# The second FFN's weight conversions in two parts, one more of them in the first group, and the last four turns in two pairs

## The chip, the cores and the metric

The program runs on one core of a Trainium2 chip. The core has a matrix engine (PE, with its weight loads shown as PEld), a vector engine (DVE), a scalar engine (ACT), a third elementwise engine that also issues gathers (POOL), and a queue engine that issues transfers (SP). The metric is the device time of one execution in microseconds (us), the median of several.

## What is computed

Three stages follow one another. The input of the third stage is x, 4608 tokens of 512 numbers, and its weights are an FFN of 2048 hidden numbers.

```
attn:  kv = k^T v per head; out = q kv; out / rms(out) * g_norm      (8 x 8 heads, 576 tokens, 64)
moe:   tokens with x @ w_skip > 0 go to one of 8 experts e:
       y = gate * (max(x @ w1[e], 0) @ w2[e]);  x = x + y             (512 -> 1024 -> 512)
moe2:  h = x @ w_in;  g = h * sigmoid(h);  out = g @ w_out            (512 -> 2048 -> 512)
```

## The kernel before, in words

Every float32 matrix product is made of three products of reduced-precision parts: high by high, high by low, low by high. So each weight and each activation is first split into two parts. The order of all work is written out by hand: each engine takes its instructions in the order in which the code issues them, and waits at the head of its queue.

The change lies in one loop, `for n in range(len(steps) + LAG)` (line 1554 on). Steps 0 to 63 are the eight experts `u` = 0 to 7 with eight weight chunks `f` = 0 to 7 each. Steps 64 to 111 are three groups of 512 tokens in the second FFN, with sixteen chunks each. A step does, in this order:

- in the experts, at `f` = 5, 6, 6, 7 one **turn** each (`turn`, line 1207): PE transposes a quarter of the next expert's rows into a PSUM tile `pt`, ACT copies the high part (L1215), DVE subtracts for the low part (L1216). There are two `pt` tiles, so the transposes of the third turn wait for the L1216 of the first. In the last expert all four turns stand at `f` = 7;
- `first` (line 1290): PE's first product of the step into `ph` (L1303), from which ACT and DVE make the two parts of the hidden tile `h` (L1309 and L1310 for an expert, L1315 to L1317 for a group);
- `split_on` (line 213): the end of the conversions that have begun, see below;
- `second` (line 1346) of the step before: PE's second product into `acc` (L1355). It needs `h` of the step before. After an expert's last chunk, DVE adds `acc` to the rows `xe` (L1365), and POOL stores them and gathers the rows of the expert after the next (L967);
- the step's preparation of later weights (`split`, line 182). An expert's chunk is one ACT copy (L187) and one DVE subtraction (L188). Half a chunk of the second FFN comes as 64-bit numbers and is **converted**: L197 on ACT and five DVE operations, L198, L200, L202, L206 and L210; later `split_on` issues an ACT copy L221, two POOL operations L222 and L223, and then a DVE addition L218.

Which half is converted at which expert step is said by the table `at_step`; the halves that remain are converted by `split_slowly(LAST_OPS)`, which advances the generator `split` by so many yields in a step of the groups. Loads of the weights run three ahead in three `stg` buffers, in the order of the conversions. Temporary tiles of a conversion (`x1`, `x2`, `x3`) are of the pool `xp` with six buffers.

Of the kernel before, what the change touches and what calls it, by code (L numbers as in the profile page):

```python
# [24 lines left out]
def tile_kernel(ctx, tc, q, qr, k, kr, v, vr, g_norm, w_skip, w_gate, we, wf, out):  # L25
    nc = tc.nc
    B, _, H, _, D = k.shape
    NT, DM = out.shape
    S = NT // B
    E, KE = we.shape[:2]  # L30
# [12 lines left out]
    KD = DM // P  # L43
# [9 lines left out]
    NW = 16  # L53
    NWE = 5
# [39 lines left out]
    NE = E * KE  # L94
# [81 lines left out]
    def part(task):  # L176
        c, half = task
        w = chunk_tile(c)
        return w if half is None else w[:, :, half * DM:(half + 1) * DM]

    def split(task):


        t = staged.pop(task)
        w = part(task)
        if task[1] is None:
            nc.scalar.activation(w[:, 0, :], t.bitcast(F32), AF.Copy)  # L187
            nc.vector.tensor_tensor(w[:, 1, :], t.bitcast(F32), w[:, 0, :].bitcast(F32), ALU.subtract)  # L188
            yield
            return  # L190
        tv = t.rearrange("p (n o) -> p n o", o=2)
        hi, lo = tv[:, :, 1], tv[:, :, 0]
        vec = nc.vector
        x1 = xp.tile([P, DM], F32, tag="x", name="x1")
        x3 = xp.tile([P, DM], F32, tag="x", name="x3")
        x2 = xp.tile([P, DM], F32, tag="x", name="x2")
        nc.scalar.activation(x3, lo.bitcast(U32), AF.Copy, scale=2.0 ** -52)  # L197
        vec.tensor_scalar(x2.bitcast(I32), hi, 0x7FFFFFFF, None, ALU.bitwise_and)  # L198
        yield
        vec.scalar_tensor_tensor(x1, x2, SMALLEST, hi.bitcast(F32), ALU.is_ge, ALU.mult)  # L200
        yield
        vec.tensor_scalar(  # L202
            x2.bitcast(I32), x1.bitcast(I32), 3, 0x3FFFFFFF, ALU.logical_shift_left, ALU.bitwise_and
        )
        yield
        vec.scalar_tensor_tensor(  # L206
            x1.bitcast(I32), x1.bitcast(I32), -0x40000000, x2.bitcast(I32), ALU.bitwise_and, ALU.bitwise_or
        )
        yield
        vec.tensor_scalar(x2.bitcast(I32), x1.bitcast(I32), -0x800000, None, ALU.bitwise_and)  # L210
        begun.append((w, x1, x2, x3))
        yield
# [12 lines left out]

    NCW = 2 * (NW - NWE)
    at_step = {}
    for n in range(NE - NWA):  # L230
        at_step.setdefault(n + 1, []).append((n + NWA, None))
    for i in range(NCW):
        n = (i // 3) * KE + 2 + 2 * (i % 3) if i < NCW - 1 else NE - KE - 1
        at_step.setdefault(n, []).append((NE + i // 2, i % 2))

    LAST_OPS = 4
    order = [(c, None) for c in range(NWA)] + [x for n in sorted(at_step) for x in at_step[n]]
    order += [(NE + i // 2, i % 2) for i in range(NCW, 2 * KF)]
    nload = [0]
    nsplit = [0]  # L240

    def load_ahead():
        while nload[0] < min(nsplit[0] + 3, len(order)):
            load_task(order[nload[0]])
            nload[0] += 1

    def split_next(n):
        for _ in range(n):
            for _ in split(order[nsplit[0]]):
                pass  # L250
            nsplit[0] += 1
            load_ahead()

# [22 lines left out]
    with ExitStack() as actx:  # L276
# [583 lines left out]
        for nb in range(3, B):  # L860
            o = {3: 2, 4: 1}.get(nb, 0)
            for i, parts in enumerate(((0, 1), (2, 3), (4,), (5,))):
                b, u = (nb - 1, o + i) if o + i < 4 + (nb - 1) % 2 else (nb, 0)
# [110 lines left out]
    for u, (kind, i) in enumerate(units):  # L974
        n = CAPS[i] if kind == "e" else GN
# [46 lines left out]
    with ExitStack() as vctx:  # L1022
        oc = vctx.enter_context(tc.tile_pool(name="oc", bufs=1))
        ps_v = vctx.enter_context(tc.tile_pool(name="ps_v", bufs=1, space=PSUM))
        with tc.For_i(0, count, 1) as _:
            vec = nc.vector
            _, _, over = reach(oc)
# [10 lines left out]
            at = oc.tile([P, NTILE, E], F32, name="at")  # L1038
# [162 lines left out]
    def turn_tile(u, kk, s, pt):  # L1201
        m = tokens_of[u][s]
        c0 = kk * (XQ if u < E else P)
        nc.tensor.transpose(pt[:, s * P:s * P + m], rows_of[u][s][0:m, c0:c0 + P], ident[0:m, 0:m])  # L1204

    def turn(u, kk, pt=None):
        if pt is None:
            pt = ps_t.tile([P, GN], F32, tag="t", name="pt")
            for s in range(len(tokens_of[u])):
                turn_tile(u, kk, s, pt)  # L1210
        if kk % 2 == 0:
            two_x[0] = xtp.tile([P, 2, 2, GN], F32R, tag="xT", name="xT")
        x = two_x[0][:, :, kk % 2]
        n = sum(tokens_of[u])
        nc.scalar.activation(x[:, 0, 0:n], pt[:, 0:n], AF.Copy)  # L1215
        nc.vector.tensor_tensor(x[:, 1, 0:n], pt[:, 0:n], x[:, 0, 0:n].bitcast(F32), ALU.subtract)  # L1216
        xT_of[u, kk] = x
# [77 lines left out]
    def first(u, f, c):  # L1295
        kind, _ = units[u]
        n = sum(tokens_of[u])
        w = chunks[c]
        ph = ps_h.tile([P, GN], F32, tag="h", name="ph")
        for kk in range(KD):  # L1300
            x = xT_of[u, kk]
            for a, (wi, xi) in enumerate(((0, 0), (0, 1), (1, 0))):
                nc.tensor.matmul(  # L1303
                    ph[:, 0:n], w[:, wi, kk * P:(kk + 1) * P], x[:, xi, 0:n],
                    start=(kk == 0 and a == 0), stop=(kk == KD - 1 and a == 2),
                )
        h = hp_.tile([P, 2, GN], F32R, tag="h", name="h")
        if kind == "e":
            nc.scalar.activation(h[:, 0, 0:n], ph[:, 0:n], AF.Relu)  # L1309
            nc.vector.scalar_tensor_tensor(  # L1310
                h[:, 1, 0:n], ph[:, 0:n], 0.0, h[:, 0, 0:n].bitcast(F32), ALU.max, ALU.subtract
            )
        else:
            sg = sgp.tile([P, GN], F32, tag="sg", name="sg")
            nc.scalar.activation(sg, ph, AF.Silu)  # L1315
            nc.scalar.activation(h[:, 0, :], sg, AF.Copy)  # L1316
            nc.vector.tensor_tensor(h[:, 1, :], sg, h[:, 0, :].bitcast(F32), ALU.subtract)  # L1317
        return h
# [243 lines left out]
    for n in range(len(steps) + LAG):  # L1562
        now = steps[n] if n < len(steps) else None
        if now is not None:
            u, f, c = now
            kind, i = units[u]
            nxt = u + 1
            if u < E:
                at = (5, 6, 6, 7) if u != E - 1 else (7, 7, 7, 7)
                for kk in range(KD):  # L1570
                    if at[kk] == f:
                        turn(nxt, kk)
            hs[n] = first(u, f, c)
        else:
            sup = super_group(0)
            for _ in range(2):
                next(sup)
        split_on()
        if n >= LAG:
            u2, f2, c2 = steps[n - LAG]  # L1580
            second(u2, f2, c2, hs.pop(n - LAG))
            last = f2 == nf[units[u2][0]] - 1
            if last and u2 + 2 <= E:
                fetch(u2 + 2)
            if u2 == E + NPL - 1 and f2 >= KF - NWE:
                load_entry(f2 - (KF - NWE))
        split_next(len(at_step.get(n, [])))
        if n >= NE:
            split_slowly(LAST_OPS)
        if now is not None and E <= u < E + NPL - 1:  # L1590
            if f < 2 * GT:
                fetch_blocks(nxt, f)
            if f >= KF - GT - 1 and f < KF - 1:
                turn_blocks(nxt, f - (KF - GT - 1))
        if now is not None and u == E + 1:
            keep_part(c, 0)
            keep_part(c, 1)
        if n >= NE + KF and (n - NE - KF) % 3 == 0 and (n - NE - KF) // 3 < KJ:
            sums_now.append(sums_of((n - NE - KF) // 3))
        for _ in range(2):  # L1600
            step_on(sums_now)
        if now is not None and u == E + NPL - 1:
            if f in (9, 10, 11, 12):
                pace(rooms[0][0])
            for v in (E + NPL, E + NPL + 1):
                if f < 4:
                    fetch_blocks(v, f)
                elif f in (9, 10, 11, 12):
                    fetch_blocks(v, f - 5)
            if f in (8, 10, 12, 14):  # L1610
                rooms.append([xp.tile([P, DM], F32, tag="x", name="room") for _ in range(4)])
                parts.append(operand_parts(E + NPL, f // 2 - 4, rooms[-1]))
            for _ in range(2):
                step_on(parts)
            assert f < KF - 1 or not parts
        if now is not None and nxt == E and f == at[0] - 1:
            sort_rows(nxt)
        if n == 0:
            row_of_place()
        elif n % 2 == 0 and n // 2 <= NP:  # L1620
            permute(n // 2 - 1)
        if n == 31:
            prepare_blocks()
        if n == 32:
            order_blocks()
        if n == 24:
            nc.sync.dma_start(inew, perm.rearrange("(p t) c -> p t c", p=P))
# [61 lines left out]
```

## Time and profile before

| what | value |
|---|---|
| median of 3 runs | 1195.29 us (1193.83 to 1196.43) |
| profiled execution | 1185.35 us, span 1183.3 us, mean granted PE clock 0.978 |
| PE busy | 1131.6 us (96%) |
| DVE, ACT, POOL busy | 595.2 us (50%), 484.0 us (41%), 368.8 us (31%) |
| experts (steps 0 to 63) | 141 to 406 us of the span |
| first group (steps 64 to 79) | about 406 to 491 us of the span |

The span is from the first instruction to the last. PE is the engine with hardly any idle time; what counts is therefore where PE waits and for whom. The other engines are idle for half the time on the average, but they work in bursts, and what they finish late can hold PE. Granted clock 1.00 is 2.4 GHz, 0.50 is 1.2 GHz.

### The profile page before, as it was taken

To read this page: it belongs to the slowest core of one execution; us is meant where nothing else is said; L and a number is where in the kernel's file an instruction comes from. 1 tells how busy PE (TensorE), PEld (TensorE's weight loads), DVE (VectorE), ACT (ScalarE), POOL (GpSimd) and SP (SyncE) were. 2 spreads that over 40 slices of the span, in tenths; PEclk is the share of its full clock that TensorE was granted. 3 is DMA by queue.
4 is the path that set the end of the run, shared out by engine and by line. 5 is a ranking of instruction groups with operands and counts; after the bars stand their busy time and mean duration, and the time that the engine had idled before them with its cause. 6 is when DMAs were issued, how large, how long until landed. Compare 5 with 4: busy or idle time off the path is not lost.

```text
span 1183.3 us, 16638 instructions
## 1 busy us (share of the span) xinstructions
PE 1131.6 (96%) x6259; PEld 939.5 (79%) x6259; DVE 595.2 (50%) x1105; ACT 484.0 (41%) x951; POOL 368.8 (31%) x369
## 2 busy tenths in 40 slices
PE   8895699999998999989999999999999999999998
PEld 7785698888886888868878788888888888888886
DVE  2467677788888577624535522355222453223222
ACT  3575354445444443422423444433244432344221
POOL 3679344535444186150063234120043200000000
PEclk9897799999999999999999999999999999999999
DMA  9867656666665433094641376432566322654202
GB/s 341 329 259 296 222 166 210 223 218 210 224 209 200 161 108 115 14 309 155 208 143 54 127 265 216 176 124 91 182 219 221 141 107 104 217 189 170 104 36 71
DMA packets 65265, 211.05 MB, mean 178 GB/s; under 512 B 9840, under 2 KB 24688, under 8 KB 53024
## 3 DMA queue, kind: packets, MB, share of 16 engines
q1 hardware_dynamic: 55760, 189.44, 45.8%
q0 software_dynamic: 8064, 20.48, 5.9%
q8 instruction: 50, 0.82, 0.3%
q10 hardware_dynamic: 1360, 0.05, 0.1%
q14 instruction: 31, 0.25, 0.1%
HBM read 162.67 MB, written 47.27 MB: 177 GB/s over the span
## 4 chain that ended last, share of the span: by engine, by line
PE 87%; DVE 5%; issue 3%; DMA 2%; ACT 2%; POOL 1%; SPq 0%; POOLq 0%; DVEq 0%; ACTq 0%
PE acc L1498 22%; PE acc L1355 19%; PE ph L1303 19%; PE pa L1451 11%; PE pc L1451 6%; PE pb L1451 3%; PE po L456 2%; PE kv L424 1%; PE pt L1204 1%; DVE w L188 1%; POOL x L223 1%; PE kv L426 1%; PE busy L1120 1%; PE G L445 0%; DMA xs<-rows 0%
## 5 line engine op out<-in xcount | busy, mean ns | idle before, releaser
L1355 PE MATMUL acc<-w,h 128*128 128x512 f32 x1128 | 282.4, 397 | 10.7 <-issue 5.5
L1303 PE MATMUL ph<-xT,w 128*128 128x512 f32 (+7 forms) x1344 | 265.8, 347 | 0.8 <-DVE w L188 0.4
L1498 PE MATMUL acc<-entry,h 128*128 128x512 f32 x1152 | 265.1, 392 | 0.0
L1498 PEld LDWEIGHTS acc<-entry,h 128*128 128x128 f32 x1152 | 216.3, 188 | 47.9
L1355 PEld LDWEIGHTS acc<-w,h 128*128 128x128 f32 x1128 | 203.4, 183 | 60.8 <-issue 7.5
L1303 PEld LDWEIGHTS ph<-xT,w 128*128 128x128 f32 x1344 | 225.3, 189 | 30.8 <-DVE w L188 0.7
L1001 POOL DMA_INDIRECT x<-xs,qidx x128 | 128.2, 1002 | 112.8 <-DVE room L1266 48.8
L1451 PE MATMUL pa<-b,entry 128*128 128x512 f32 x576 | 141.8, 393 | 0.0
L1479 DVE TENSOR_TENSOR h<-g,h 128x512 fp32r<-128x512 f32 x96 | 66.5, 693 | 147.8 <-ACT h L1478 145.4
L1451 PEld LDWEIGHTS pa<-b,entry 128*128 128x128 f32 x576 | 108.2, 188 | 24.8
L1478 ACT ACTIVATE h<-g 128x512 fp32r<-128x512 f32 x96 | 60.5, 630 | 146.6 <-PE acc L1498 141.5
L1317 DVE TENSOR_TENSOR h<-sg,h 128x512 fp32r<-128x512 f32 x48 | 34.8, 726 | 119.4 <-ACT h L1316 81.0
L188 DVE TENSOR_TENSOR w<-stg_None,w 128x1024 fp32r<-128x1024 f32 x64 | 80.3, 1256 | 17.3 <-ACT w L187 15.7
L1433 ACT ACTIVATE g<-g 128x512 f32<-128x512 f32 x72 | 45.4, 633 | 103.1 <-DVE g L1431 91.0
L1315 ACT ACTIVATE sg<-ph 128x512 f32<-128x512 f32 x48 | 28.7, 597 | 141.7 <-PE ph L1303 102.4
L222 POOL TENSOR_TENSOR x<-x,x 128x512 f32<-128x512 f32 x32 | 41.6, 1299 | 111.3 <-DVE x L210 106.1
L1451 PE MATMUL pc<-b,entry 128*128 128x512 f32 x288 | 74.3, 393 | 0.0
L1309 ACT ACTIVATE h<-ph 128x304 fp32r<-128x304 f32 (+6 forms) x64 | 28.0, 437 | 109.0 <-PE ph L1303 97.1
L187 ACT ACTIVATE w<-stg_None 128x1024 fp32r<-128x1024 f32 x64 | 67.1, 1049 | 9.8 <-DMA xs<-rows 9.8
L1451 PEld LDWEIGHTS pc<-b,entry 128*128 128x128 f32 x288 | 54.1, 188 | 12.4
L223 POOL TENSOR_TENSOR x<-x,w 128x512 f32<-128x512 f32 x32 | 62.9, 1966 | 0.6 <-ACT w L221 0.6
L1431 DVE TENSOR_TENSOR g<-pc,u 128x512 f32<-128x512 f32 x24 | 16.6, 692 | 73.0 <-PE pc L1451 73.0
(216 smaller groups left out, 1166.8 us busy)
## 6 DMA issues: line engine op xcount, KB each, us to landing
entry<-wa SPq DMA_DIRECT2D x42, 1024.0 KB
stg_None<-in_we_dram SPq DMA_DIRECT2D x64, 512.0 KB
entry<-wb SPq DMA_DIRECT2D x24, 1024.0 KB
stg<-in_wf_dram SPq DMA_DIRECT2D x32, 512.0 KB
xs<-rows SPq DMA_DIRECT2D x8, 1032.0 KB
wb<-w SPq DMA_DIRECT2D x16, 512.0 KB
wa<-parts SPq DMA_DIRECT2D x32, 256.0 KB
k<-in_k_dram SPq DMA_DIRECT2D x7, 1024.0 KB
```

The costliest lines, as they stand in the source:

```text
L187: nc.scalar.activation(w[:, 0, :], t.bitcast(F32), AF.Copy)
L188: nc.vector.tensor_tensor(w[:, 1, :], t.bitcast(F32), w[:, 0, :].bitcast(F32), ALU.subtract)
L222: nc.gpsimd.tensor_tensor(x3, x3, x2, ALU.mult)
L223: nc.gpsimd.tensor_tensor(x1, x1, w[:, 0, :].bitcast(F32), ALU.subtract)
L1001: nc.gpsimd.indirect_dma_start(out=rows_of[u][s][:, a * XQ:(a + 1) * XQ], out_offset=None, in_=xblocks, in_offset=bass.IndirectOffsetOnAxi ...
L1303: nc.tensor.matmul(ph[:, 0:n], w[:, wi, kk * P:(kk + 1) * P], x[:, xi, 0:n], start=(kk == 0 and a == 0), stop=(kk == KD - 1 and a == 2),)
L1355: nc.tensor.matmul(accs[u, s][0:m], h[:, hi, s * P:s * P + m], w[:, wi, DM:2 * DM], start=(f == 0 and a == 0), stop=(last and a == 2),)
L1433: nc.scalar.activation(g, acc, AF.Silu)
L1451: nc.tensor.matmul(p, w[:, wi, kk], x[:, xi, kk], start=(i in FIRST_IN_BANK and kk == 0 and a == 0), stop=(kk == 1 and a == 2), skip_group ...
L1478: nc.scalar.activation(h[:, 0], g, AF.Copy)
L1479: nc.vector.tensor_tensor(h[:, 1], g, h[:, 0].bitcast(F32), ALU.subtract)
L1498: nc.tensor.matmul(acc[ni, s], h[:, hi, s * P:(s + 1) * P], w[:, wi], start=(j == 0 and fi == 0 and a == 0), stop=(last and a == 2),)
```

## The change

Three things are changed. First, the table `at_step` holds 21 halves in place of 22, at `f` = 0, 2 and 4 of experts 0 to 6 (before: `f` = 2, 4, 6 and one more at step 55), and each is issued in two parts: ACT's L197 and DVE's L198, L200, L202 at its step, L206 and L210 at the next step (`split_at`). Second, eleven halves in place of ten are left for the first group, and `LAST_OPS` is 5 in place of 4, which is a whole conversion in each of the steps 64 to 74. Third, in the last expert two of the four turns go behind `first` of step 63.

```diff
-    NCW = 2 * (NW - NWE)
+    NCW = 2 * (NW - NWE) - 1
...
-        n = (i // 3) * KE + 2 + 2 * (i % 3) if i < NCW - 1 else NE - KE - 1
-        at_step.setdefault(n, []).append((NE + i // 2, i % 2))
-
-    LAST_OPS = 4
+        at_step.setdefault((i // 3) * KE + 2 * (i % 3), []).append((NE + i // 2, i % 2))
+
+    LAST_OPS = 5
...
+    parted = []
+
+    def split_at(n):
+
+        while parted:
+            for _ in parted.pop():
+                pass
+        for task in at_step.get(n, []):
+            g = split(order[nsplit[0]])
+            if task[1] is None:
+                for _ in g:
+                    pass
+            else:
+                for _ in range(3):
+                    next(g)
+                parted.append(g)
+            nsplit[0] += 1
+            load_ahead()
...
-                for kk in range(KD):
+                for kk in range(KD if u != E - 1 else KD // 2):
                     if at[kk] == f:
                         turn(nxt, kk)
             hs[n] = first(u, f, c)
+            if u == E - 1 and f == at[0]:
+                for kk in range(KD // 2, KD):
+                    turn(nxt, kk)
...
-        split_next(len(at_step.get(n, [])))
+        split_at(n)
```

DVE's queue in expert 6 before, from the chunk subtraction of step 48 on (`w50` is an expert's chunk, `stg73_0` half a chunk of the second FFN, `h` a step's hidden tile):

```order
L188 TENSOR_TENSOR w50_4215<-stg50_None_4127,w50_4215 128x1024
L1310 SCALAR_TENSOR_TENSOR h_4233<-ph_4220,h_4233 128x288
L188 TENSOR_TENSOR w51_4248<-stg51_None_4138,w51_4248 128x1024
L1310 SCALAR_TENSOR_TENSOR h_4266<-ph_4253,h_4266 128x288
L188 TENSOR_TENSOR w52_4278<-stg52_None_4177,w52_4278 128x1024
L198 TENSOR_SCALAR x2_4286<-stg73_0_4218 128x512
L200 SCALAR_TENSOR_TENSOR x1_4284<-x2_4286,stg73_0_4218 128x512
L202 TENSOR_SCALAR x2_4286<-x1_4284 128x512
```

The same place now (line numbers of the changed kernel; its L1328 is L1310 of before):

```order
L188 TENSOR_TENSOR w50_4215<-stg50_None_4095,w50_4215 128x1024
L198 TENSOR_SCALAR x2_4223<-stg73_0_4141 128x512
L200 SCALAR_TENSOR_TENSOR x1_4221<-x2_4223,stg73_0_4141 128x512
L202 TENSOR_SCALAR x2_4223<-x1_4221 128x512
L1328 SCALAR_TENSOR_TENSOR h_4243<-ph_4230,h_4243 128x288
L206 SCALAR_TENSOR_TENSOR x1_4221<-x1_4221,x2_4223 128x512
L210 TENSOR_SCALAR x2_4223<-x1_4221 128x512
L188 TENSOR_TENSOR w51_4260<-stg51_None_4178,w51_4260 128x1024
L1328 SCALAR_TENSOR_TENSOR h_4278<-ph_4265,h_4278 128x288
L188 TENSOR_TENSOR w52_4293<-stg52_None_4218,w52_4293 128x1024
```

The conversion has moved two steps up, and it stands on both sides of an `h`. Three of its operations now come right behind the additions to `xe`, which stand ahead of the first row.

DVE's queue at the start of the first group before, from `h` of step 65 to the conversion that begins at step 66:

```order
L1317 TENSOR_TENSOR h_4833<-sg_4834,h_4833 128x512
L210 TENSOR_SCALAR x2_4811<-x1_4809 128x512
L198 TENSOR_SCALAR x2_4862<-stg75_1_4669 128x512
L200 SCALAR_TENSOR_TENSOR x1_4860<-x2_4862,stg75_1_4669 128x512
L202 TENSOR_SCALAR x2_4862<-x1_4860 128x512
L1317 TENSOR_TENSOR h_4882<-sg_4883,h_4882 128x512
L218 TENSOR_TENSOR w75_4808<-x1_4809,x3_4810 128x512
L206 SCALAR_TENSOR_TENSOR x1_4860<-x1_4860,x2_4862 128x512
L210 TENSOR_SCALAR x2_4862<-x1_4860 128x512
```

The same place now (its L1335 is L1317 of before):

```order
L1335 TENSOR_TENSOR h_4818<-sg_4819,h_4818 128x512
L218 TENSOR_TENSOR w74_4373<-x1_4793,x3_4794 128x512
L198 TENSOR_SCALAR x2_4848<-stg75_0_4654 128x512
L200 SCALAR_TENSOR_TENSOR x1_4846<-x2_4848,stg75_0_4654 128x512
L202 TENSOR_SCALAR x2_4848<-x1_4846 128x512
L206 SCALAR_TENSOR_TENSOR x1_4846<-x1_4846,x2_4848 128x512
L210 TENSOR_SCALAR x2_4848<-x1_4846 128x512
L1335 TENSOR_TENSOR h_4870<-sg_4871,h_4870 128x512
L218 TENSOR_TENSOR w75_4845<-x1_4846,x3_4847 128x512
```

Before, the closing addition L218 of a conversion stood behind the first operations of the next one. Now L218 of a conversion stands ahead of all five operations of the next, in every step.

## Rows read from the trace of the kernel before

**Rows 1.** PE's waits in the experts, 135 to 410 us: waiter, releaser, total, times, longest

```profile
PE pt L1204 <- DVE xT L1216: 3.1, 3, 1.6
PE acc L1355 <- DVE xe L1365: 1.8, 1, 1.8
PE acc L1355 <- DVE h L1310: 1.2, 1, 1.2
```

**Rows 2.** Busy time of two stretches: PE, PEld, DVE, ACT, POOL (instructions), PE clock, DMA

```profile
47.00:60.00 13.00, 10.61 (x172) 9.13 (x170) 7.37 (x25) 5.90 (x19) 9.58 (x9) 1.00 0.67 249
381.30:388.10 6.80, 6.22 (x20) 5.25 (x21) 5.33 (x9) 1.33 (x2) 2.56 (x3) 0.50 0.61 175
```

**Rows 3.** Timeline, expert 6, steps 52 and 53 (start, duration, engine, operation, idle before)

```profile
360.31 1.22 DVE L188 TENSOR_TENSOR w<-stg_None,w 128x1024 fp32r<-128x1024 f32 x1
361.44 0.42 DVE L198 TENSOR_SCALAR x<-stg 128x512 int32<-128x512 int32 x1
...
363.09 0.69 DVE L206 SCALAR_TENSOR_TENSOR x<-x,x 128x512 int32<-128x512 int32 x1
...
364.16 0.42 DVE L1216 TENSOR_TENSOR xT<-pt,xT 128x256 fp32r<-128x256 f32 x1
364.49 0.45 DVE L1310 SCALAR_TENSOR_TENSOR h<-ph,h 128x288 fp32r<-128x288 f32 x1
364.63 0.44 PE L1204 MATMUL pt<-ident,xe 128*128 128x128 f32 x2 [0.52 <-DVE xT L1216]
365.43 1.33 DVE L188 TENSOR_TENSOR w<-stg_None,w 128x1024 fp32r<-128x1024 f32 x1 [0.49 <-ACT w L187]
365.63 2.28 POOL L223 TENSOR_TENSOR x<-x,w 128x512 f32<-128x512 f32 x1
```

**Rows 4.** Timeline, the same expert's start, step 48

```profile
341.52 1.75 PE L1303 MATMUL ph<-xT,w 128*128 128x288 f32 x12
345.06 2.05 DVE L1365 SCALAR_TENSOR_TENSOR xe<-acc,xe 128x512 f32<-128x512 f32 x3
351.10 0.97 POOL L967 DMA_INDIRECT xe<-xs,gidx  x1 [0.31 <-issue]
356.19 1.75 PE L1303 MATMUL ph<-xT,w 128*128 128x288 f32 x12
```

**Rows 5.** Timeline, first and third turn of experts 2 and 5

```profile
232.52 0.48 DVE L1216 TENSOR_TENSOR xT<-pt,xT 128x320 fp32r<-128x320 f32 x1
233.26 1.15 PE L1204 MATMUL pt<-ident,xe 128*128 128x128 f32 x6
332.13 0.45 DVE L1216 TENSOR_TENSOR xT<-pt,xT 128x288 fp32r<-128x288 f32 x1
332.30 1.10 PE L1204 MATMUL pt<-ident,xe 128*128 128x128 f32 x6
```

**Rows 6.** Timeline, first group: one conversion from its POOL part to the next

```profile
436.75 1.30 POOL L222 TENSOR_TENSOR x<-x,x 128x512 f32<-128x512 f32 x1
...
439.33 0.69 DVE L218 TENSOR_TENSOR w<-x,x 128x512 fp32r<-128x512 f32 x1 [2.74 <-POOL x L223]
439.94 0.42 DVE L198 TENSOR_SCALAR x<-stg 128x512 int32<-128x512 int32 x1
442.20 0.68 DVE L1317 TENSOR_TENSOR h<-sg,h 128x512 fp32r<-128x512 f32 x1
443.37 1.33 POOL L222 TENSOR_TENSOR x<-x,x 128x512 f32<-128x512 f32 x1 [0.99 <-DVE x L210]
443.59 1.66 DVE L200 SCALAR_TENSOR_TENSOR x<-x,stg 128x512 f32<-128x512 f32 x1
```

**Rows 7.** Timeline, first group: the first POOL part, and second products of steps 66 and 75

```profile
417.74 1.30 POOL L222 TENSOR_TENSOR x<-x,x 128x512 f32<-128x512 f32 x1
423.52 2.88 PE L1355 MATMUL acc<-w,h 128*128 128x512 f32 x12
472.56 2.91 PE L1355 MATMUL acc<-w,h 128*128 128x512 f32 x12
```

## The prediction

> **What bounds the kernel now.** I read the totals first: PE is busy for 96% of the span, so only PE's own waits can be won or lost. The list of waits says for the experts where they are [rows 1]: 3.1 us for L1216, in three waits; 1.8 us for the additions to `xe`; 1.2 us for `h`. All three releasers are DVE, though DVE is busy for half the span only: its bursts are the matter. The longest of the 3.1 is 1.6 us (expert 1); the second, 0.52 us, is in expert 6 at 364.63 [rows 3]; the rest, 1.0 us, are the four turns of expert 7, whose third needs a `pt` tile. The 1.8 and 1.2 us lie together at 378 to 382 us, where expert 6's last two conversions meet the end of the expert. Then the clock: from 381.3 to 388.1 us the granted clock is 0.50, right behind those two waits, and PE is busy for 6.22 us of it [rows 2]. The work of half of that, 3.1 us, is lost. So the experts hold 6.1 + 3.1 = 9.2 us that a better order of DVE could win. In the first group the list of waits has no wait of PE for DVE at all.
>
> **Last turns in two pairs.** The third turn no longer asks at once for the tile of the first; PE has step 63's first product to do meanwhile. The 1.0 us goes. DVE does `h` of step 63 and then the last two subtractions while PE does the second product of step 62. **-1.0 us**, with -0.5 and -1.0 as bounds.
>
> **The old stalls of the experts.** Expert 6 loses two conversions at its end (`f` = 6 and 7), so the waits at 378 to 382 us and the slow clock behind them go: 1.8 + 1.2 + 3.1 = 6.1 us. Expert 1's and expert 6's waits at the turns (1.6 + 0.5) belong to the next part. **-6.1 us.**
>
> **New lateness at the first turn.** DVE's work in an expert stays the same, but up to the first turn there is more of it, and it starts behind the three additions to `xe`. I walk through expert 6. Prices by start to start [rows 3]: L188 1.13 us (360.31 to 361.44), L198 to L202 1.65 (361.44 to 363.09), L206 and L210 1.07 (363.09 to 364.16), `h` 0.36 (0.45 less the overlap of 0.09 that L1216 and `h` show), L218 0.61 (439.33 to 439.94) [rows 6]. A conversion's POOL part is two operations of about 1.25 us. What happens when DVE and POOL overlap is shown by two pairs of rows: L200, 0.69 us alone, took 1.66 when it came 0.2 us behind L222 [rows 6]; L223, 1.30 alone, took 2.28 when L188 was ahead of it [rows 3]. So one waits for the other's end, whoever comes second.
> Step 48: the additions start at 345.06 [rows 4] and take 2.0; L188 to 348.2; L198 to L202 to 349.8. Step 49: `h` to 350.2, L206 and L210 to 351.3, L188 to 352.4. POOL's gathers are done at 351.10 + 0.97 = 352.1 [rows 4]; L222 waits for L188 and runs from 352.5 to 353.7. Step 50: `h` to 352.8; L188 stands behind L222, 353.7 to 354.9; L223 came next, to 356.0; L198 to L202 behind it, to 357.6. Step 51: `h` to 358.0. PE wants it at the end of step 52's first product, 356.19 + 1.7 = 357.9 [rows 4]: just in time. L218, L206, L210, L188: to 360.8. Step 52: `h` to 361.1; the conversion's L222 to 362.0 holds up L188, to 363.2; L223 to 364.3 holds up L198 to L202, to 366.0. Then the first turn's L1216 starts at 366.0; before, it started at 364.16 [rows 3], so it is 1.8 us later, and PE, which wanted the tile at 364.1 and waited 0.52, waits 2.3.
> The other experts have the same pattern, 1.8 us later, against what slack they had. In expert 2, L1216 was done at 233.0, and the third turn's transposes came at about 233.7 (half-way through the six from 233.26): slack 0.7, new wait 1.1. In expert 5 it was 332.6 against 332.7: 1.7 [rows 5]. Experts 3 and 4 between these: 1.4 and 1.5. Expert 1, whose old wait came from POOL's late gathers, keeps some 0.6; expert 0 has no additions and no wait. Together 8.6 us, for which the 2.1 of the old waits go: +6.5 net. The walk lets no operation slip between two of POOL; I take a little less, **+5.4 us**. Bounds: -2.1 (DVE is evenly loaded and PE never waits) and +8 us.
> The mean L188 behind a POOL operation was hardly longer (1.33 against 1.22) [rows 3]; by this row alone the wait for POOL costs 0.1 us each time and there would be no new wait, which is the lower bound. The Trainium skill (SBUF — State Buffer, "Who interferes with whom") speaks against that: a DVE instruction with two SBUF inputs and a GpSimd instruction that reads SBUF exclude each other for the whole of the first one. The two stretched rows agree with it. By it the sum of this part is the walk's +6.5 us.
>
> **One more conversion in the first group, five operations a step.** Now L218 of a conversion stands ahead of all five operations of the next. That makes a closed chain: L210, then L222 (it reads L210's result), L223, L218, then the next five operations, then `h`, then L222 again. The trace has one turn of just this chain, with one `h` in it: from L222 at 436.75 to L222 at 443.37, 6.62 us, with DVE never idle from L218 on and POOL never idle before it [rows 6]. A step of PE is 5.44 us (472.56 - 423.52 = 49.04 over nine steps) [rows 7]. Before, the four yields a step made one conversion in 1.25 steps, 6.8 us, and the chain just fitted. Now it does not, and each step of DVE takes 1.2 us longer than PE's.
> Where it starts: the first L222 cannot be earlier than 417.74 [rows 7], since POOL's queue has the first gathers of the group ahead of it, which wait for expert 7's stores. `h` of step k+1 ends when L222 of the conversion of step k starts, at 417.74 + 6.6 (k - 64). For step 66 that is 424.3; PE's second product wants it at 423.52 [rows 7]: 0.8 us late already. For step 75, behind the conversion of step 74, it is 483.7 against 472.56: **+11.2 us**. PE cannot hide it, as every second product waits for `h`. Bounds: if `h` runs while POOL works and costs the chain nothing, the turn is about 6.1 us, and step 75's `h` comes at 478.7: +6.2. If the stretched `x` operations recur and the turned blocks of step 75 come on top: +13.
>
> **Sum.** -1.0 - 6.1 + 5.4 + 11.2 = **+9.5 us** on the profiled 1185.35 us. The runs' median is 9.9 us above the profiled one for reasons that this trace does not show; I add the difference to the median: 1195.29 + 9.5 = **1204.8 us**.
>
> **Rivals.**
> *Faster.* DVE is evenly loaded and the chain is short. For it: the odd steps of before had DVE idle while it waited for ACT's copy behind L221, and L221 no longer waits. Against it: the walk. With no new turn waits the experts and the turns give -9.2; the chain at its lower bound gives +6.2: -3.0, 1192.3 us. If the chain took less than 5.5 us a turn, all -9.2 would stay: 1186.1. It decides at a turn of 6.1 us together with clean turns.
> *No change.* The turns are clean (-9.2) but the chain is full (+11.2): +2.0, 1197.3 us, within 0.2%, which is about what a measurement of this kernel can tell from no change.
> *Slower by the clock too.* The many waits in a row pull the granted clock down, as those at 378 to 382 us did. Each such stretch costs about 3.1 us [rows 2]; one or two give 1208 to 1211 us. Against it: from 47 to 60 us PE was busy for 10.61 of 13 us, 82%, at clock 1.00 [rows 2], and 5.44 of 6.6 is the same share.
>
> **How the numbers follow.** The forecast has 0.53, the clock rival 0.16, no change 0.15, faster 0.16. So slower 0.69, same 0.15, faster 0.16. The range leaves out the faster case and the far end of the clock: 1194 to 1213 us. The forecast's own range is 1199 to 1209.
>
> **What would show it.** In steps 66 to 75, PE waits for DVE's `h` (L1317) at each second product, about 1.1 us each, and nowhere else in the group; L222 follows L222 at 6.5 to 6.7 us. In experts 2 to 6, PE waits once each at the third turn's transposes for L1216, 1 to 2.3 us; at expert 6's end there is no wait and no slow clock; no wait among the last four turns. Wrong would be: a turn of the chain under 5.5 us, `h` on time in the group, or turns without a wait.

## The result and the profile after

The changed kernel takes 1202.06 us in the median of 13 runs (1192.96 to 1205.17), the kernel before, run beside it, 1195.29 us in 13 (1190.80 to 1201.19). The ratio is 1.0053, with a 95% interval of 1.0035 to 1.0071: the change makes the kernel 4.2 to 8.5 us slower.

The first table is worked out from PE's rows in each trace, with the same marks: the experts last from the first product of step 0 to that of step 64, the first group to that of step 80, the second to that of step 96, and the third to the next part's first product (us).

| kernel | experts | group 1 | group 2 | group 3 | the rest | span |
|---|---|---|---|---|---|---|
| before | 265.24 | 86.18 | 95.50 | 91.46 | 504.35 | 1183.3 |
| changed | 260.15 | 96.74 | 94.32 | 101.87 | 504.36 | 1201.2 |

Ahead of the experts lie 140.6 and 143.8 us. The experts win 5.1 us and the first group loses 10.6: +5.5 us, which is within the interval of the ratio. The span of the profiled execution grew by far more, 17.9 us, where the median grew by 6.8. Of the 17.9 us, 10.4 lie in group 3 and 3.2 ahead of the experts. Ahead of the experts the time differs without the change as well: five_alone, whose code is that of before up to step 64, has 144.8 us there. The last conversion ends at 483.7 us, in the first group. In groups 2 and 3 PE waited in the kernel before too, at other places (2.2 us for ACT, and 5.5 us for which the trace names no releaser), and four kernels further down had no such wait. So the stages are compared, not the spans.

PE's waits in the experts of the changed kernel, 135 to 410 us (waiter, releaser, total, times, longest), which answer to [rows 1]:

```profile
PE pt L1222 <- DVE xT L1234: 3.5, 4, 1.0
...
PE ph L1321 <- DVE w L188: 0.7, 2, 0.5
```

The waits for `xe` and for `h` are gone, and the granted clock is 1.00 from 137 to 543 us. It is so in the stretch that had 0.50 before, too (columns as in [rows 2]):

```profile
381.30:388.10 6.80, 6.80 (x43) 5.82 (x42) 5.15 (x7) 3.14 (x5) 1.46 (x2) 1.00 0.77 234
```

At the turns PE waits for 1.03 us in expert 1 (1.63 before), 1.01 in expert 3 and 0.75 in expert 5 (none before), and 0.70 in expert 6 (0.52 before). The last four turns show no wait.

The same view in the first group, 400 to 495 us, where PE had no wait for DVE before:

```profile
PE acc L1373 <- DVE h L1335: 6.5, 10, 0.7
PE acc L1373 <- ACT h L1334: 0.5, 1, 0.5
```

One step of the first group in the timeline of the changed kernel (start, duration, engine, operation, idle time before and its releaser; [rows 6] has the old one):

```profile
434.24 0.61 PE L1373 MATMUL acc<-w,h 128*128 128x512 f32 x2
434.44 0.43 DVE L210 TENSOR_SCALAR x<-x 128x512 int32<-128x512 int32 x1
434.78 0.69 DVE L1335 TENSOR_TENSOR h<-sg,h 128x512 fp32r<-128x512 f32 x1
435.01 1.60 POOL L222 TENSOR_TENSOR x<-x,x 128x512 f32<-128x512 f32 x1 [0.52 <-DVE x L210]
435.52 2.60 PE L1373 MATMUL acc<-w,h 128*128 128x512 f32 x10 [0.67 <-DVE h L1335]
436.58 1.29 POOL L223 TENSOR_TENSOR x<-x,w 128x512 f32<-128x512 f32 x1
437.90 0.69 DVE L218 TENSOR_TENSOR w<-x,x 128x512 fp32r<-128x512 f32 x1 [2.44 <-POOL x L223]
438.51 0.42 DVE L198 TENSOR_SCALAR x<-stg 128x512 int32<-128x512 int32 x1
...
440.88 0.43 DVE L210 TENSOR_SCALAR x<-x 128x512 int32<-128x512 int32 x1
441.23 0.69 DVE L1335 TENSOR_TENSOR h<-sg,h 128x512 fp32r<-128x512 f32 x1
441.46 1.60 POOL L222 TENSOR_TENSOR x<-x,x 128x512 f32<-128x512 f32 x1 [0.52 <-DVE x L210]
```

The reader is to see that this circle has no slack. L222 waits for L210, L218 waits for L223 while DVE is idle for 2.44 us, and then `h` stands behind five operations with nothing idle ahead of it. L222 follows L222 after 6.45 us. PE's wait names only the last link, DVE's `h`; the idle times on DVE and POOL name the circle.

Expert 6 in the changed kernel, from the additions at its start to the late turn (the columns are the same; [rows 3] and [rows 4] have the old ones):

```profile
347.71 1.75 PE L1321 MATMUL ph<-xT,w 128*128 128x288 f32 x12
350.32 2.05 DVE L1383 SCALAR_TENSOR_TENSOR xe<-acc,xe 128x512 f32<-128x512 f32 x3
358.70 1.29 POOL L223 TENSOR_TENSOR x<-x,w 128x512 f32<-128x512 f32 x1
359.53 1.54 DVE L188 TENSOR_TENSOR w<-stg_None,w 128x1024 fp32r<-128x1024 f32 x1 [1.58 <-ACT w L187]
364.77 2.14 POOL L222 TENSOR_TENSOR x<-x,x 128x512 f32<-128x512 f32 x1 [4.78 <-DVE x L210]
366.09 1.91 DVE L188 TENSOR_TENSOR w<-stg_None,w 128x1024 fp32r<-128x1024 f32 x1
366.87 2.28 POOL L223 TENSOR_TENSOR x<-x,w 128x512 f32<-128x512 f32 x1
367.92 1.52 DVE L198 TENSOR_SCALAR x<-stg 128x512 int32<-128x512 int32 x1
370.54 0.42 DVE L1234 TENSOR_TENSOR xT<-pt,xT 128x256 fp32r<-128x256 f32 x1
371.01 0.44 PE L1222 MATMUL pt<-ident,xe 128*128 128x128 f32 x2 [0.70 <-DVE xT L1234]
```

At 364.77 to 369.44 us the two engines alternate: L188 has to wait for L222, L223 for L188, L198 for L223, and each is longer by about 0.7 to 1.1 us than alone (1.22, 1.30, 0.42). They don't always alternate. In expert 3 an L188 stood behind both POOL operations and took 3.28 us, though it had been waiting when L223 began, and PE waited 0.45 us for it:

```profile
258.62 1.31 POOL L222 TENSOR_TENSOR x<-x,x 128x512 f32<-128x512 f32 x1
258.98 3.28 DVE L188 TENSOR_TENSOR w<-stg_None,w 128x1024 fp32r<-128x1024 f32 x1 [2.31 <-issue]
259.88 1.28 POOL L223 TENSOR_TENSOR x<-x,w 128x512 f32<-128x512 f32 x1
```

Experts 2, 4 and 5 have such an L188 each, of 3.00, 2.52 and 2.96 us. What decides which of two waiting operations goes first, these rows don't show.

### The profile page after: what moved, and what is told of

Read it like the earlier page. It is cut to its first block, busy times and chain, and to the rows that moved or that the text cites. A ratio compares the mean times of both kernels' runs of the same rounds, so it can differ in the third digit from the quotient of the medians.

```text
span 1201.2 us, 16634 instructions
## 1 busy us (share of the span) xinstructions
PE 1140.7 (95%) x6259; PEld 943.0 (79%) x6259; DVE 601.8 (50%) x1105; ACT 484.0 (40%) x951; POOL 375.4 (31%) x369
## 4 chain that ended last, share of the span: by engine, by line
PE 75%; DVE 11%; issue 4%; POOL 3%; ACT 3%; DMA 2%; another core or an unknown queue 2%; SPq 0%; DVEq 0%; POOLq 0%; ACTq 0%
PE acc L1516 22%; PE ph L1321 13%; PE acc L1373 13%; PE pa L1469 11%; PE pc L1469 6%; PE pb L1469 3%; DVE w L188 2%; PE po L474 2%; DVE x L200 2%; PE kv L442 1%; DVE x L198 1%; POOL rows L625 1%; POOL x L223 1%; DVE x L206 1%
## 5 line engine op out<-in xcount | busy, mean ns | idle before, releaser
L1373 PE MATMUL acc<-w,h 128*128 128x512 f32 x1128 | 287.1, 400 | 15.7 <-DVE h L1335 6.5
L188 DVE TENSOR_TENSOR w<-stg_None,w 128x1024 fp32r<-128x1024 f32 x64 | 94.5, 1477 | 14.3 <-ACT w L187 10.8
L1335 DVE TENSOR_TENSOR h<-sg,h 128x512 fp32r<-128x512 f32 x48 | 33.1, 690 | 119.1 <-ACT h L1334 99.4
L222 POOL TENSOR_TENSOR x<-x,x 128x512 f32<-128x512 f32 x32 | 57.5, 1795 | 78.9 <-DVE x L210 78.8
L187 ACT ACTIVATE w<-stg_None 128x1024 fp32r<-128x1024 f32 x64 | 67.4, 1054 | 25.1 <-DMA stg_None<-in_we_dram 15.8
L625 POOL TENSOR_TENSOR rows<-rows,grow 128x512 f32<-128x512 f32 x36 | 41.7, 1181 | 36.8 <-ACT rows L487 36.8
```

The source lines that it names most:

```text
L222: nc.gpsimd.tensor_tensor(x3, x3, x2, ALU.mult)
L625: nc.gpsimd.tensor_tensor(xv, xv, f.to_broadcast([P, HP, 2, D]), ALU.mult)
L1373: nc.tensor.matmul(accs[u, s][0:m], h[:, hi, s * P:s * P + m], w[:, wi, DM:2 * DM], start=(f == 0 and a == 0), stop=(last and a == 2),)
```

## The experiments

Each kernel was profiled, and those with a ratio were timed in several rounds against the kernel before on the same chip. The stage times are read as in the table above (experts, then group 1):

| kernel | experts | group 1 | time, and the ratio to before (95%) |
|---|---|---|---|
| four_ops | 259.53 | 86.27 | 1184.65, 0.9958 (0.9929 to 0.9986) |
| five_alone | 265.47 | 94.80 | 1201.95, 1.0097 (1.0069 to 1.0125) |
| late_close | 260.90 | 91.78 | 1188.38, 0.9979 (0.9958 to 0.9999) |
| pool_cut | 254.34 | 96.87 | 1184.66, one run |
| turns_alone | 263.27 | 86.17 | 1173.56, one run |
| late_cut | 259.93 | 86.18 | 1168.61, one run |
| four_135 | 257.09 | 86.29 | 1167.79, 0.9915 (0.9887 to 0.9943) |
| four_136 | 255.08 | 86.28 | 1164.89, 0.9903 (0.9875 to 0.9931) |
| whole_024 | 280.94 | 86.29 | 1208.75, one run |
| whole_136 | 256.80 | 86.29 | 1177.26, one run |

The kernel before took 1189.40 us beside the first four, 1177.66 beside the next four and 1182.24 beside the last two; times of different sets can't be compared directly. The times that the expectations name start from 1195.29 us or from four_ops; only the differences can be held against what was measured.

**four_ops: the first group's rate alone.** Against the changed kernel:

```diff
-    LAST_OPS = 5
+    LAST_OPS = 4
```

> The changed kernel with four operations a step in the first group, as before, in place of five; the 21 conversions in two parts over the experts and the last turns in two pairs stay. Chain theory (the closing addition ahead of all five operations of the next conversion closes a chain of 6.4 to 6.6 us against PE's step of 5.44 us): the eleven conversions then take 1.25 steps each, no second product waits for h by more than 0.3 us, steps 64 to 79 last 86 to 87.5 us in place of 96.7, and the time is 5 us under that of before, 1189 to 1192 us. Rival (one conversion more is what costs, however it is paced): steps 64 to 79 keep 3 us or more of the loss, time 1194 us or more.

Group 1 lasts 86.27 us, as before the change, and PE has no wait in it. The experts keep their gain. By its ratio this version beats both kernels: the parts of the change that concern the experts are worth 5.7 - 0.1 = 5.6 us by the stages, and 0.42% by the ratio, 5.0 us of 1189.4.

**five_alone: the same number in the kernel before.**

```diff
-    LAST_OPS = 4
+    LAST_OPS = 5
```

> The kernel before with five operations a step in the first group and nothing else; ten conversions are left for the group. Chain theory: about 1.0 us in each of nine second products from step 66 to 74, steps 64 to 79 last 95 to 96 us in place of 86.2, time 9 to 10 us above before, 1204 to 1206 us. Rival (the loss of the changed kernel comes from the experts, whose lateness is carried into the group): steps 64 to 79 last under 89 us, time within 3 us of before.

Group 1 loses 8.6 us with nothing else changed, a little less than expected, and the ratio gives 8.2 to 14.9 us for the whole kernel. PE's list for 400 to 505 us has the same waits:

```profile
PE acc L1355 <- DVE h L1317: 5.9, 9, 0.7
```

Nine waits in place of ten, since ten halves were left and not eleven. Together with four_ops this settles that the loss comes from the five operations a step.

**late_close: the circle opened at L218.** The exhausted generator no longer issues L218 itself, so L218 comes one step later, behind the next `h`:

```diff
             if next(slow[0], slow) is slow:
                 slow.clear()
-                split_on()
                 load_ahead()
```

> The changed kernel, where the closing additions of the first group's conversions are issued one step later, behind the next step's h, in place of right ahead of the next conversion; five operations a step stay, and so does all work of DVE and POOL. Chain theory: the closed chain is open, L222 of one conversion runs beside the operations of the next; most of the loss of 10.5 us in steps 64 to 79 goes (86 to 90 us in place of 96.7), time 1190 to 1195 us. Rival (DVE and POOL exclude each other, and 4.0 us of DVE and 2.5 us of POOL a step are more than 5.44): the loss of about 1 us a step stays, steps 64 to 79 last 95 us or more, time 1200 us or more.

Of the 10.6 us that group 1 had lost, 5.0 came back and 5.6 stayed. So neither expectation came true: 91.8 us lies between the theory's 86 to 90 and the rival's 95 or more. PE's list for 400 to 500 us:

```profile
PE acc L1372 <- DVE h L1334: 2.8, 8, 0.4
```

One round of its timeline, from `h` to `h`, shows what still binds:

```profile
445.37 0.68 DVE L1334 TENSOR_TENSOR h<-sg,h 128x512 fp32r<-128x512 f32 x1
445.60 1.61 POOL L222 TENSOR_TENSOR x<-x,x 128x512 f32<-128x512 f32 x1 [0.41 <-issue]
445.97 1.78 DVE L218 TENSOR_TENSOR w<-x,x 128x512 fp32r<-128x512 f32 x1
447.16 1.74 POOL L223 TENSOR_TENSOR x<-x,w 128x512 f32<-128x512 f32 x1
447.67 1.51 DVE L198 TENSOR_SCALAR x<-stg 128x512 int32<-128x512 int32 x1
449.22 0.69 DVE L200 SCALAR_TENSOR_TENSOR x<-x,stg 128x512 f32<-128x512 f32 x1
...
451.48 0.68 DVE L1334 TENSOR_TENSOR h<-sg,h 128x512 fp32r<-128x512 f32 x1
```

DVE is not idle between these rows, and `h` still follows `h` only after 6.11 us. L218 lasts 1.78 us where it is 0.69 alone, L198 1.51 where it is 0.42: both end behind a POOL operation. The prediction had 6.1 us as the chain's lower bound, but for another reason: there `h` was to run beside POOL and cost nothing, while here DVE has no idle time at all. So the two numbers agree without the reason being the same. The stages give +1.3 us for this kernel, while the ratio's interval says 0.1 to 5.0 us faster; that difference of a few us isn't explained.

**late_cut: late_close without POOL's time in the groups.**

```diff
-            nc.gpsimd.tensor_tensor(x3, x3, x2, ALU.mult)
-            nc.gpsimd.tensor_tensor(x1, x1, w[:, 0, :].bitcast(F32), ALU.subtract)
+            z = 1 if step_no[0] >= NE else DM
+            nc.gpsimd.tensor_tensor(x3[:, 0:z], x3[:, 0:z], x2[:, 0:z], ALU.mult)
+            nc.gpsimd.tensor_tensor(x1[:, 0:z], x1[:, 0:z], w[:, 0, 0:z].bitcast(F32), ALU.subtract)
```

(`NE` is 64, the number of the experts' steps, and `DM` is 512.)

> As late_close, and POOL's two operations of a conversion cover one column in place of 512 in the steps of the groups (these weights are then not the low parts that they should be; nothing else is left out). late_close still had 5.6 us more in the first group than the kernel before (91.8 against 86.2), with a step of about 6.1 us. Theory: with the chain open, what fills a step is that DVE and POOL wait for each other's ends: DVE's five operations, L218 and h are 3.7 us, POOL's two 2.5, together 6.2. Then the first group falls to 86 to 87 us here and has no wait for h. Rival: DVE's queue alone is too full or is held by ACT's copies (L197, L221) between its operations: the group stays at 90 us or more.

Group 1 lasts 86.18 us, exactly that of before, and has no wait of PE. The busy times from 429 to 484 us say why (columns as in [rows 2]: PE, PEld, DVE, ACT, POOL). The changed kernel, then late_close, then late_cut:

```profile
429.00:484.00 55.00, 49.53 (x207) 38.19 (x208) 31.98 (x59) 18.45 (x32) 38.37 (x28) 1.00 0.31 100
```

```profile
429.00:484.00 55.00, 52.17 (x220) 40.36 (x219) 52.31 (x69) 20.20 (x41) 37.67 (x27) 1.00 0.30 94
```

```profile
429.00:484.00 55.00, 55.00 (x242) 45.19 (x242) 34.04 (x70) 22.99 (x49) 12.66 (x21) 1.00 0.26 81
```

DVE's 69 operations of late_close took 52.31 us, 95% of the stretch; 70 of late_cut took 34.04. The difference, 18 us, was DVE waiting for POOL, booked as busy. So the loss has two causes of like size: the wait for L218 at the head of the queue (5.0 us) and, when that is gone, the two engines that exclude each other (5.6). In the changed kernel itself DVE is busy for only 31.98 us: there the first cause hides the second.

**pool_cut: no POOL time in the experts.** The same edit of the changed kernel, with the condition turned round (one column in the experts' steps, all in the groups).

> The changed kernel, where the two POOL operations of each of the 21 conversions in the experts work on one column of 512; their results, and with them the second FFN's weights, are not what they should be. The order of all queues stays. Theory of the shared wait (DVE's lateness at the first turn comes from waiting for POOL's two operations): the waits of PE at the third turn's transposes (1.03, 1.02, 0.75, 0.70 us in experts 1, 3, 5, 6) go, all of them under 0.2 us, and the experts last 256 to 257.5 us in place of 260.2. Rival (more DVE work ahead of the first turn, behind the additions to xe): half of these waits or more stays.

The experts last 254.34 us, and PE's list from 135 to 395 us has no wait for DVE at all:

```profile
PE ph L1323 <- ACT xT L1235: 0.3, 1, 0.3
PE pt L1224 <- issue: 0.2, 1, 0.2
```

That is 5.8 us less than the changed kernel, more than was expected, and group 1 is as long as ever (96.87). So, by this one trace, the waits at the turns come from POOL's two operations of a conversion, not from DVE's own work.

**turns_alone: the last turns in the kernel before.**

```diff
-                for kk in range(KD):
+                for kk in range(KD if u != E - 1 else KD // 2):
...
+            if u == E - 1 and f == at[0]:
+                for kk in range(KD // 2, KD):
+                    turn(nxt, kk)
```

> The kernel before with the last four turns in two pairs around step 63's first product, and nothing else of the change. By the prediction's first step the 1.0 us wait of PE at the third turn of expert 7 (401 us) goes and nothing comes for it: the experts last 264.2 us in place of 265.2, and the rest of the trace is as before. Rival: the wait only moves, to step 64's first product, which now comes right behind the last two turned tiles: the experts stay at 265.2 us with a new wait of 0.5 to 1.0 us at 403 to 406 us.

The wait at the third turn (1.0 us) is gone, and none came at step 64. The experts are 2.0 us shorter. Steps 62 and 63, where the edit is, give 1.4 of it: the wait had cost more than its row says. The other 0.6 is at step 57, ahead of the edit: there the slow stretch of the clock lasted 3.41 us in this run and 6.82 before, while a wait for L188 was 0.9 us longer.

**four_135 and four_136: other places for the conversions.** four_ops with other chunks in the table:

```diff
-        at_step.setdefault((i // 3) * KE + 2 * (i % 3), []).append((NE + i // 2, i % 2))
+        at_step.setdefault((i // 3) * KE + 1 + 2 * (i % 3), []).append((NE + i // 2, i % 2))
```

> As four_ops (four yields a step in the groups), and the 21 halves stand at chunks 1, 3 and 5 of the experts in place of 0, 2 and 4. If what was late at the turns is the work of POOL and DVE on three conversions ahead of the first turn (at chunk 5), the third conversion now comes behind that turn and its POOL part behind all turns but the last: the waits at the turns of experts 1, 2, 4 and 5 (1.0, 1.0, 0.8, 0.7 us in four_ops) fall under 0.3 each, the experts last 256 to 257.5 us in place of 259.5, and the time is 1181 to 1183 us where four_ops has 1184.7. Rival: what matters is the total in an expert, and the third conversion now meets the additions to xe and h at the expert's end, as in the kernel before at 378 to 382 us: waits of 1 to 3 us there in some experts, experts 261 to 265 us, and a time of 1187 to 1190 us.

and, for four_136, `(i // 3) * KE + (1, 3, 6)[i % 3]`:

> As four_135, with the third half at chunk 6 in place of 5. By the theory the turns are at least as clean as in four_135, and the price is paid at the end of an expert, where L206 and L210 now stand at chunk 7 and POOL's part in the next expert's first step, ahead of POOL's gathers: experts 256 to 260 us. Rival: nothing stands in POOL's or DVE's way there (POOL's gathers wait for the stores anyway): the same as four_135 within 1 us.

The experts fall to 257.1 and 255.1 us; the rest of group 1 stays whole. In four_135 three waits are left at turns: 0.94 and 0.30 us in expert 1, the first of them longer than expected, and 0.34 in expert 6. The rival of four_135, a collision at the expert's end, didn't come. In four_136 PE's waits for DVE from 135 to 500 us are these:

```profile
PE pt L1222 <- DVE xT L1234: 0.4, 1, 0.4
...
PE ph L1321 <- DVE xT L1234: 0.2, 1, 0.2
```

The third conversion's POOL part now runs behind all four turns, and the price at the expert's end that the expectation named didn't come either; the experts are 2.0 us shorter than in four_135, where the rival had them within 1. four_136 has the lowest ratio, though its interval overlaps that of four_135: 0.97% less than the kernel before, 11.4 us of 1177.66, against 10.1 us by the stages.

**whole_024 and whole_136: each conversion in one part.** four_ops and four_136 with all five operations at their step again:

```diff
-            if task[1] is None:
-                for _ in g:
-                    pass
-            else:
-                for _ in range(3):
-                    next(g)
-                parted.append(g)
+            for _ in g:
+                pass
```

> As four_ops (21 halves at chunks 0, 2 and 4, four yields a step in the groups, last turns in two pairs), but each conversion whole at its step: L206 and L210 stand ahead of the next h again. If the parting gives DVE's h its place in time, undoing it makes h late behind the five operations: new waits of PE for h of 0.3 to 1 us in several experts, and the experts last 261 to 264 us in place of 259.5. Rival: the parting does nothing by itself, since DVE's h was not on the edge in the steps that follow chunks 0, 2 and 4; the whole gain at the expert's end comes from the places: experts 259 to 260 us with the same waits for L1234 at the third turn.

> As four_136, but each conversion whole at its step. If the parting matters, h of the next step is late behind the third conversion at chunk 6, which stands between the turns, and behind that at chunk 3: waits of 0.5 to 1.2 us for h or L188, experts 257 to 261 us in place of 255.1. Rival: the places do it all: experts 255 to 256 us and no new wait over 0.3 us.

At chunks 0, 2 and 4 the parting is decisive: without it the experts last 280.9 us, far beyond what either theory gave. PE's list for 135 to 424 us in whole_024:

```profile
PE pt L1217 <- DVE xT L1229: 9.6, 6, 2.0
PE acc L1368 <- DVE h L1323: 4.5, 5, 1.0
PE ph L1316 <- DVE w L188: 4.2, 4, 1.8
```

That is 18.3 us of waits, and three slow stretches of the clock besides, which were not in the expectation. At chunks 1, 3 and 6 the parting is worth little: two waits for L188, 1.2 us together, and experts of 256.8 us, 1.7 more than four_136, which is what neither expectation had. Each is one run, so its sum is not an interval, but the waits are in the trace.

## Why the prediction was right, and which term was off

The time came out within the forecast's own range, and all four terms have the sign that was predicted. Three came within 0.8 us of it, and one was 2.2 us too large. To size them, the lengths of PE's steps (from one step's first product to the next one's) are compared in the two traces:

| term | predicted | measured | read from |
|---|---|---|---|
| last turns | -1.0 | -1.4 | steps 62 and 63 |
| old stalls | -6.1 | -6.9 | steps 57 and 58 |
| new lateness at the turns | +5.4 | +3.2 | experts 0 to 6 |
| closed chain | +11.2 | +10.6 | first group |
| sum | +9.5 | +5.5 | |

Every term came out lower than predicted, so no error made up for another.

**Last turns.** Right: no wait among the turns, and turns_alone shows it by itself. The 0.4 us beyond the wait's row was not in the sum.

**Old stalls.** Right: expert 6's end has neither wait nor slow clock. A wait of 0.4 us for L188 there, which the sum had left out, went with them.

**New lateness at the turns.** This is the term that was mis-sized. By the waits that PE shows it is +2.1 us: 3.5 at the turns and 0.7 for L188, less 2.1 of old ones. By the steps it is +3.2: 2.1 in expert 3, 0.8 in expert 5, and at most 0.2 either way in each of the others. The mechanism holds: pool_cut takes all of these waits away. Of the signs named, two came out weaker: experts 2 and 4 have no wait at the third turn, and the waits of experts 3, 5 and 6 are 0.7 to 1.0 us in place of 1 to 2.3.

The walk went wrong in two places, which expert 6 shows. First, it let the additions to `xe` start where they had started before, 345.06 - 341.52 = 3.54 us behind step 48's first product [rows 4]. But there they stood behind an L218 of the conversion at chunk 6, and that conversion is gone. Now they start 350.32 - 347.71 = 2.61 us behind it: 0.9 us of slack that the walk didn't count. Second, the walk had the first conversion's POOL part alternate with DVE's L188 and L198. In the trace it fell into 1.58 us in which DVE waited for ACT's copy (L187), so L223 was out of L198's way. From the additions to the first turn's subtraction the walk had 366.0 - 345.06 = 20.9 us; it took 370.54 - 350.32 = 20.2. So 2.3 - 0.9 - 0.7 = 0.7 us, the wait that PE shows.

The first point holds in experts 1 to 6: counted from the expert's first product, the additions start 0.7 to 1.5 us earlier than before. The second doesn't hold in experts 2 to 5, where an L188 met the first conversion's POOL part (2.5 to 3.3 us, above). Counted from the first product of chunk 5, the first turn's subtraction came 0.9, 1.8, 0.4, 1.0 and 0.2 us later than before in experts 2 to 6, where the walk had 1.8 in each. Why these differ so wasn't followed row by row.

The term's lower bound rested on a row misread. The L188 of 1.33 us came at 365.43 [rows 3], when an L222 of the kernel before was nearly over, so it shows only the end of a wait:

```profile
364.39 1.29 POOL L222 TENSOR_TENSOR x<-x,x 128x512 f32<-128x512 f32 x1 [4.72 <-DVE x L210]
```

**Closed chain in the first group.** Right. The first L222 of the group in the changed kernel's timeline:

```profile
415.98 1.31 POOL L222 TENSOR_TENSOR x<-x,x 128x512 f32<-128x512 f32 x1
```

It came 415.98 - 403.91 = 12.1 us behind step 64's first product; the prediction had 417.74 - 405.81 = 11.9. A round takes 6.45 us, not 6.6, and PE's waits are 0.4 to 0.7 us where 1.1 was named, though a step grew by about 1.0. What the prediction saw as one chain is two limits on top of each other, as late_close and late_cut show: opening the chain leaves rounds of 6.1 us, in which DVE and POOL wait for each other's ends, as in the two stretched rows of before.

**The rivals.** The granted clock stayed at 1.00 through all ten waits of the group, so the clock rival fell. The turns were cleaner than forecast, part of the way to the rivals "faster" and "no change", but the chain was full: the sum by the stages, +5.5 us, lies between the forecast and "no change". The rule of the Trainium skill (SBUF — State Buffer, "Who interferes with whom") that a DVE instruction with two SBUF inputs and a GpSimd instruction that reads SBUF exclude each other is borne out: in late_close L218 lasted 1.78 us in place of 0.69 beside L222. L198 has one input and was stretched as well, to 1.51 us in place of 0.42; the same section counts `tensor_scalar` among the operations that can take the shared port in its two-port modes, and the trace agrees.

## What to carry to other kernels

When work is spread in pieces over the steps of a busier engine, add up the round trip through all engines that it visits, not the busy share of each: here DVE was busy for half the span, and one more piece a step made a circle of 6.45 us against a step of 5.44. By these rows, count DVE's two-input work and POOL's elementwise work as if they ran on one engine, and place the pieces so that POOL's part falls where DVE's next result isn't awaited: with the third conversion's behind the turns (four_136) one wait of 0.4 us was left there; with it ahead of them there were four, of up to 1 us each. A gain and a loss in one change can be read apart by stages, and each can then be kept or dropped alone.

## What the runs showed beyond that

A wait of PE cost more than its row says. In group 1 of the changed kernel a step lasts 444.38 - 437.96 = 6.42 us, against 5.45 before (49.04 us over nine steps [rows 7]): 0.97 us more, with a shown wait of 0.67. The twelve matmuls of a second product take 2.9 us in one piece [rows 7], and 0.61 + 2.60 = 3.21 us when they wait after the second. So some 0.3 us come on top of each wait in that place.

In groups 2 and 3 PE waited for ACT by up to 7.1 us at a time (4.4 and 4.3 in the changed kernel; the 7.1 of whole_136 is shown below). The four kernels timed beside 1177.66 us, all on one chip, took 87.56 us for each of these groups and had no such wait. All the other eight traces have waits there, and six of them are known to be from two other chips. ACT's own idle time carries no name of the program, "remote":

```profile
525.16 0.60 ACT L1328 ACTIVATE sg<-ph 128x512 f32<-128x512 f32 x1 [14.29 <-remote]
```

In the 7 us ahead, 512 to 519 us, the DMA engines were busy for 95% (the last column but one). But so they were, for 99%, in the same place of four_136, 28 us behind step 80's first product, where nothing waited:

```profile
512.00:519.00 7.00, 7.00 (x32) 5.81 (x31) 0.00 (x0) 0.00 (x0) 5.19 (x6) 1.00 0.95 284
510.00:517.00 7.00, 7.00 (x32) 5.81 (x31) 0.69 (x1) 1.23 (x2) 5.20 (x6) 1.00 0.99 289
```

So busy DMA engines alone don't explain it. What held ACT there wasn't tried, and stays open.

The granted clock fell in some places behind waits and not in others. The ten waits of 0.4 to 0.7 us in the changed kernel's group 1 left it at 1.00. In whole_024 it was 0.50 for 3.41 us each at 244, 319 and 357 us, each time 1 to 2 us behind the end of a wait at the turn (1.34 to 1.60 us) that had a wait for `h` (0.85 to 0.98 us) some 8 us ahead of it. Behind the like pairs of expert 1 (0.81 and 1.67 us, at 198 and 206 us) and expert 3 (0.93 and 1.47 us, at 273 and 281 us) it stayed at 1.00. What makes the difference, these rows don't show.
